# Geglu feed-forward and attention on TensorE's two row halves: rows and weights in 3.5 pieces of 128, worked in two phases

## The chip, the core and the metric

The kernel runs on one core of a Trainium2 chip. The metric is the device time of one execution in microseconds (us), as the median of several runs. Beside it there is one profiled execution, with its trace. The engines are called as in the profile: PE is TensorE's matmul, PEld its weight load, DVE VectorE, ACT ScalarE, POOL GpSimd, SP SyncE, which here only issues DMAs.

## The reference

One input `x` of 2048 rows and 448 columns goes through a layernorm without gain. The result feeds two branches, whose product is added to `x`. All inputs are bfloat16.

```python
xn = _layernorm(x)                                   # 2048 x 448
# branch A: attention, 16 query heads of 256, 8 key/value heads, the last W = 512 keys
q = (xn @ wq).reshape(B, Sq, Hq, Dh)                 # wq: 448 x 4096
scores = einsum("bhqd,bhkd->bhqk", q, k) * Dh ** -0.5
s = (softmax(scores) @ v).reshape(B, Sq, Hq * Dh) @ wo
# branch B: feed-forward, F = 1792
g = _silu((_gelu(xn @ w_gate) * (xn @ w_up)) @ w_down)
return x + s * g
```

## The kernel before

The rows are worked in four chunks (`c`) of 512, each of four tiles (`t`) of 128 rows. Two products contract over the 448 columns of `xn`: gate/up and Q. 448 is seven times 64, and so the kernel splits TensorE's 128 rows into two halves. A matmul uses 64 rows and 128 columns of the array, and the two halves run side by side on different work, each with its own PSUM bank. The transposed `xnT` therefore holds seven pieces of 64 rows, and holds each of them twice, in partitions 0 to 63 and in 64 to 127. The gate weights lie in the lower half of `wgu` and the up weights in the upper half; `wq` has one head of a pair in each half.

**Recording and order.** Every operation goes through `Rec.op` (line 65), which writes down for each engine a list in program order, and finds by keys such as `("ps", bank)` on which earlier operations it depends. Each engine runs its own list strictly in this order; a dependence on another engine becomes a semaphore wait (`emit`, line 98). A dependence of a TensorE operation on an earlier one of TensorE is left out. DMAs are issued from SP (`q1` in the profile) or POOL (`q0`), and they too wait in their issuing engine's list.

**Start.** Four loads bring the first chunk of `x`; DVE takes the statistics (L288, L289), ACT the square root (L330), DVE normalises (L294). `warm` (L303) keeps TensorE busy meanwhile with 12 matmuls of zeros. `ln_tr` transposes tile by tile on TensorE (L316), 14 half transposes per tile, each tile into a bank of its own (4 to 7), and ACT (L322) or DVE (L324) copies the bank into `xnT`. For the later chunks `ln_later` (statistics on DVE, reciprocal root on POOL, L345 and L347) and `ln_later2` (L294 twice, once for each copy, and a DMA transpose from SP) are woven into the feed-forward loop of the chunk ahead: in chunk 0 from `f` = 4 on, in chunks 1 and 2 from `f` = 1 on, alternately one of each.

**Feed-forward.** For each chunk the loop over `f` (14 blocks of 128 of the 1792 columns) calls `gate_up` (L362): 14 matmuls (L370) fill bank `s` with a gate block and bank `s + 1` with the up block; ACT takes Gelu of the first (L374) and DVE multiplies the second by it (L376), into `actT`. Three pairs of banks (0 to 5) take turns. Then `down` (L379, L382) does 4 times 14 matmuls of 448 columns into banks 6 and 7. In the last chunk `down` is deferred: its matmuls fill the first slots of attention (`fill`, line 528). Weight pieces for attention are loaded by `load_piece` from POOL, each held back until a named TensorE operation is done.

**Attention.** A step is one head of one chunk (64 steps `i`), in four tiles `t`. `scores` (L420) does two matmuls into bank 4 or 5, ACT takes exp with a row sum (L424), DVE the reciprocal and the scaling (L426, L427), and an SP DMA transposes into `pT`. `values` (L440) follows some two and a half steps later, `outproj` (L460) eight steps in groups. Every four steps `q_burst` (L398) makes Q for four heads: four times 14 matmuls (L406), each 14 copied by ACT out of two banks at once (L410). Burst 0 uses bank pairs (4, 0, 2, 0), the others (0, 2, 0, 2). It stands after the first score and values of every fourth step, and the next score follows directly.

Of the kernel before, what the change touches and what calls it, by code (L numbers as in the profile page):

```python
# [11 lines left out]
P = 128  # L12
# [10 lines left out]
class Rec:  # L23
# [41 lines left out]
    def op(self, eng, fn, r=(), w=(), dma=False, after=(), lane=None):  # L65

        o = _Op(eng, fn, dma, lane)
        deps = []
        if lane is not None:
            if lane in self.lanes:  # L70
                deps.append((self.lanes[lane], True))
            self.lanes[lane] = o
        for k in (*r, *w):
            deps += [(x, True) for x in self._touch(k)]
        for k in r:
            if k in self.writer:
                deps.append((self.writer[k], True))
        for k in w:
            if k in self.writer:
                deps.append((self.writer[k], False))  # L80
            deps += [(x, False) for x in self.readers.get(k, [])]
        deps += [(x, True) for x in after]
        for d, raw in deps:
            if d.eng == eng and not d.dma and not dma and (eng == "tensor" or not raw and eng != "gpsimd"):
                continue
            d.inc = d.waited = True
            o.deps.append(d)
        for k in r:
            self.readers.setdefault(k, []).append(o)
        for k in w:  # L90
            self.writer[k] = o
            self.readers[k] = []
        if dma:
            o.inc = True
        self.ops[eng].append(o)
        return o
# [45 lines left out]
def bass_recurrent_scan__sliding_block_cached__geglu_ffn__prompt_kernel(nc, A_x, A_k, A_v, A_wq, A_wo, B_x, B_wg, B_wu, B_wd, out):  # L142
# [6 lines left out]
    QC, TPC, HP = 512, 4, 64  # L149
    NQC = S // QC  # L150
    NT = NQC * TPC
    NK = D // HP
    NF, NJ, NE = F // P, W // P, Dh // P
    assert S % QC == 0 and D % HP == 0 and NE == 2 and NJ == 4 and Hq == 2 * Hkv and Hq % 4 == 0 and NF % 2 == 0
# [4 lines left out]
    with es:  # L159
# [20 lines left out]
        xnT, _ = sb("xnT", [P, NQC, NK, QC], BF16)  # L180
# [3 lines left out]
        wq, _ = sb("wq", [P, NK, Hkv, Dh], BF16)  # L184
        wo, _ = sb("wo", [P, Hq * NE, D], BF16)
        gu_at = off[0]
        wgu, x_at = sb("wgu", [P, NK, F], BF16)
        x4, _ = sb("x4", [P, NT, D], BF16)
        NX = 4
        xn2, d_at = sb("xn2", [P, NX, NK, 2, HP], BF16)  # L190
        wd, _ = sb("wd", [P, NF, D], BF16)
        actT, hb_at = sb("actT", [P, NF, QC], BF16)
        NHB = 4
        hb, ffn_end = sb("hb", [P, NHB, QC], BF16)

# [9 lines left out]
        while at + 2 * W <= d_at:  # L205
            t_, at = sb("pr%d" % len(pr), [P, W], BF16, at)
            pr.append(t_)
        at = hb_at
        while at + 2 * W <= ffn_end:
            t_, at = sb("pr%d" % len(pr), [P, W], BF16, at)  # L210
            pr.append(t_)
# [27 lines left out]
        dve(lambda e: e.memset(actT[:, NF - 1, :], 0.0), w=[("actT", NF - 1)])  # L239
# [9 lines left out]
        wg_v = B_wg.rearrange("(k p) f -> p k f", p=HP)  # L249
        wu_v = B_wu.rearrange("(k p) f -> p k f", p=HP)  # L250
        cuts = [0, 2, 6, 10, NF]
        fslice = {f: s for s in range(4) for f in range(cuts[s], cuts[s + 1])}

        def load_gu(s):
            a, b = cuts[s] * P, cuts[s + 1] * P
            dma("sync", wgu[0:HP, :, a:b], wg_v[:, :, a:b], w=[("wgu", 0, s)])
            dma("sync", wgu[HP:P, :, a:b], wu_v[:, :, a:b], w=[("wgu", 1, s)])
# [6 lines left out]
        for sl in range(4):  # L264
# [4 lines left out]
        for c in range(2, NQC):  # L269
# [5 lines left out]
        wq_v = A_wq.rearrange("(k p) (g two m) -> p k g two m", p=HP, two=2, m=Dh)  # L275
        pieces = [(wq[lo * HP:(lo + 1) * HP, k, :, :], wq_v[:, k, :, lo, :], ("wq", lo, k))
                  for k in range(NK) for lo in range(2)]
# [13 lines left out]
        def ln_norm(t, copies=2):  # L291
            s = t % NX
            for o in range(copies):
                dve(lambda e, o=o: e.tensor_scalar(  # L294
                    xn2[:, s, :, o, :], x4[:, t, :].rearrange("p (k d) -> p k d", k=NK), mv[:, t, 0:1],
                    rstd[:, t:t + 1], op0=ALU.subtract, op1=ALU.mult),
                    r=[("x4", t), ("mv", t), ("rstd", t)], w=[("xn2", s, o)])

        def warm(n):

            def run(e):
                for _ in range(n):
                    ins = e.matmul(bank(3), lhsT=actT[:, NF - 1, 0:P], rhs=actT[:, NF - 1, :], start=True, stop=True)  # L303
# [3 lines left out]
        def ln_tr(t):  # L307
            parts = ((act, 4),), ((dve, 5),), ((act, 6),), ((dve, 7),)
            parts = [(eng, b, 0, NK) for eng, b in parts[t]]
            for eng, b, a, z in parts:  # L310
                tp = bank(b).bitcast(BF16)

                def tr(e, tp=tp, a=a, z=z):
                    for k in range(a, z):
                        for lo in (0, HP):
                            ins = e.transpose(tp[lo:lo + HP, (k - a) * P:(k - a + 1) * P], xn2[:, t, k, 0, :], ident[:, :])  # L316
                    return ins
                pe(tr, r=[("xn2", t, 0), ("ident",)], w=[("ps", b)])
                dst = xnT[:, 0, a:z, t * P:(t + 1) * P]
                src = tp[:, 0:(z - a) * P].rearrange("p (k q) -> p k q", q=P)  # L320
                if eng is act:
                    act(lambda e, dst=dst, src=src: e.activation(dst, src, ACT.Copy), r=[("ps", b)], w=[("xnT", 0, t, a)])  # L322
                else:
                    dve(lambda e, dst=dst, src=src: e.tensor_copy(dst, src), r=[("ps", b)], w=[("xnT", 0, t, a)])  # L324
# [7 lines left out]
        for a in range(0, TPC, 2):  # L332
            dve(lambda e, a=a: e.reciprocal(rstd[:, a:a + 2], std[:, a:a + 2]),
                r=[("std", a)], w=[("rstd", a), ("rstd", a + 1)])
            ln_norm(a, 1)
            ln_norm(a + 1, 1)
        warm(12)
        for t in range(TPC):
            ln_tr(t)
        xn0 = [("xnT", 0, t, 0) for t in range(TPC)]  # L340
# [9 lines left out]
        def ln_later2(t):  # L350
            c, t4 = divmod(t, TPC)
            ln_norm(t)
            dmaT(xnT[:, c, :, t4 * P:(t4 + 1) * P], xn2[:, t % NX, :, :, :].rearrange("p k a d -> p (k a d)"),
                 r=[("xn2", t % NX, 0), ("xn2", t % NX, 1)], w=[("xnT", c, t4)])

        def xn(c):
            return [("xnT", c, t) for t in range(TPC)] if c else xn0
# [4 lines left out]
        def gate_up(c, f):  # L362

            n = c * NF + f
            s = 2 * (n % NGB)

            def run(e):
                for k in range(NK):
                    for b, lo in ((s, 0), (s + 1, HP)):
                        ins = e.matmul(bank(b), lhsT=wgu[lo:lo + HP, k, f * P:(f + 1) * P],  # L370
                                       rhs=xnT[lo:lo + HP, c, k, :], start=k == 0, stop=k == NK - 1)
                return ins
            pe(run, r=xn(c) + [("wgu", 0, fslice[f]), ("wgu", 1, fslice[f])], w=[("ps", s), ("ps", s + 1)])
            act(lambda e: e.activation(hb[:, n % NHB, :], bank(s), ACT.Gelu_apprx_tanh),  # L374
                r=[("ps", s)], w=[("hb", n % NHB)])
            dve(lambda e: e.tensor_tensor(actT[:, f, :], bank(s + 1), hb[:, n % NHB, :], ALU.mult),  # L376
                r=[("ps", s + 1), ("hb", n % NHB)], w=[("actT", f)])

        def down(c, t, part=range(NF)):  # L379
            b = (6, 7, 7, 2)[t] if c == NQC - 1 else 6 + t % 2  # L380
# [15 lines left out]
        def q_burst(G):  # L396

            c, h0 = divmod(4 * G, Hq)  # L398
            for n in range(4):
                hp, e_ = divmod(n, 2)  # L400
                s, i = 2 * (n % 2) if G else (4, 0, 2, 0)[n], (4 * G + 2 * hp) % 6

                def run(e, hp=hp, e_=e_, s=s):
                    for k in range(NK):
                        for b, lo in ((s, 0), (s + 1, HP)):
                            ins = e.matmul(bank(b), lhsT=wq[lo:lo + HP, k, h0 // 2 + hp, e_ * P:(e_ + 1) * P],  # L406
                                           rhs=xnT[lo:lo + HP, c, k, :], start=k == 0, stop=k == NK - 1)
                    return ins
                pe(run, r=xn(c) + [("wq", lo, k) for lo in range(2) for k in range(NK)], w=[("ps", s), ("ps", s + 1)])
                act(lambda e, e_=e_, s=s, i=i: e.activation(  # L410
                    qT[:, i:i + 2, e_, :], psum[:, s * 512:(s + 2) * 512].rearrange("p (a q) -> p a q", a=2), ACT.Copy),
                    r=[("ps", s), ("ps", s + 1)], w=[("qT", i, e_), ("qT", i + 1, e_)])
# [93 lines left out]
        for c in range(NQC):  # L506
            lead = 4 if c == 0 else 1
            for f in range(NF):
                gate_up(c, f)
                if c + 1 < NQC and lead <= f < lead + 2 * TPC:  # L510
                    t, half = divmod(f - lead, 2)
                    (ln_later2 if half else ln_later)((c + 1) * TPC + t)
                if f >= 9 and f % 2:
                    load_piece()
            for g in ((0, 1), (2, 3, 4), (5, 6, 7), ())[c]:
# [12 lines left out]
        for d, slots in ((0, range(0, 4)), (1, range(4, 12)), (2, range(16, 20)), (3, range(20, 24))):  # L528
# [4 lines left out]
        for i in range(NI):  # L533
            for t in range(TPC):
                scores(i, t)
                if 4 * i + t in fill:
                    down(NQC - 1, *fill[4 * i + t])
                if t % 2 == 0 and 4 * i + t >= 10:
                    values(*pv.pop(0))
                if 6 <= i and t % 2:  # L540
                    outproj(*outs[0], range(2 * t - 2, 2 * t + 2))
                    if t == TPC - 1:
                        outs.pop(0)
                if t == 0 and i % 4 == 3 and i + 1 < NI:
                    q_burst(i // 4 + 1)
            if 7 <= i and (i - 7) % 3 == 0 and (i - 7) // 3 < NT:
# [43 lines left out]
```

## Time and profile before

| | |
|---|---|
| median of 3 runs | 560.89 us (560.74 to 561.54) |
| the profiled execution | 561.18 us |
| its span in the trace | 559.4 us |
| granted TensorE clock | 1.00 |
| PE busy | 549.0 us (98%) in 3499 records |
| DVE, ACT, POOL busy | 322.9, 296.1, 90.1 us |
| chain that ended last | PE 95% |
| DMA | 58.83 MB, mean 105 GB/s |

All times in a profile line are counted from the start of the span. In a line of groups stand the line of the kernel, the engine, the operation, the tiles out<-in with their sizes and the count; then the busy time in us, the mean of one in ns, and the idle time of the engine just before it with what ended that. In a line of the timeline stand the start and the length in us, then the operation and its count; the square bracket has the idle time before it. Matmuls are pipelined: the time of one in the groups (376 ns) is longer than its share in a dense sequence. The 1.78 us between span and time lie outside the program's instructions.

### The profile page before, as it was taken

How to read it: one execution, taken by the hardware profiler on the slowest of the kernel's cores; microseconds unless marked ns; L12 is line 12 of the kernel's file. 1: busy time of each engine (PE TensorE's matmuls, PEld its weight loads, DVE VectorE, ACT ScalarE, POOL GpSimd, SP SyncE). 2: the span in 40 equal slices, each digit the busy share in tenths (PEclk: the TensorE clock that was granted, in tenths of full speed). 3: DMA queues.
4: the chain of work that ended last, by engine and by line, in shares of the span. 5: the costliest groups of instructions: out<-in, count | busy, mean ns of one | idle time of the engine just before them, and what ended most of it. 6: DMA issues, size and time to landing. Idle time of an engine off the chain costs nothing.

```text
span 559.4 us, 9865 instructions
## 1 busy us (share of the span) xinstructions
PE 549.0 (98%) x3499; PEld 257.2 (46%) x3532; DVE 322.9 (58%) x835; ACT 296.1 (53%) x673; POOL 90.1 (16%) x125
## 2 busy tenths in 40 slices
PE   7999999999999999999999999999999999999997
PEld 3544444444444444444444444444444444444445
DVE  5636446143464847474846657484747484755674
ACT  4324233247655565556565656656565656565641
POOL 0232323200000111013501101232100021400023
PEclk9999999999999999999999999999999999999999
DMA  8994746972453435353664344445535353645352
GB/s 193 276 191 86 138 102 136 247 137 65 94 85 68 97 64 99 69 91 64 143 98 94 73 86 71 81 84 137 101 67 99 63 95 71 147 79 101 70 92 52
DMA packets 169552, 58.83 MB, mean 105 GB/s; under 512 B 160160, under 2 KB 166432, under 8 KB 169504
## 3 DMA queue, kind: packets, MB, share of 16 engines
q1 hardware_dynamic: 166208, 45.50, 44.2%
q0 software_dynamic: 3152, 12.65, 8.9%
q8 instruction: 28, 0.46, 0.4%
q14 instruction: 20, 0.16, 0.1%
q10 hardware_dynamic: 144, 0.06, 0.0%
HBM read 17.92 MB, written 1.84 MB: 35 GB/s over the span
## 4 chain that ended last, share of the span: by engine, by line
PE 95%; DMA 1%; DVE 1%; issue 1%; SPq 1%; ACT 0%
PE ps L440 20%; PE ps L420 19%; PE ps L406 18%; PE ps L460 16%; PE ps L370 15%; PE ps L382 8%; DMA wgu<-in_B_w_up_dram 1%; SPq L233 1%; DVE tmp L469 0%; DVE ofin L471 0%; DVE pr L427 0%; DVE oT L446 0%; DVE rden L426 0%; ACT pr L424 0%
## 5 line engine op out<-in xcount | busy, mean ns | idle before, releaser
L424 ACT ACTIVATE pr<-ps 128x512 bf16<-128x512 f32 x256 | 152.8, 597 | 116.6 <-PE ps L420 112.5
L420 PE MATMUL ps<-kT,qT 128*128 128x512 bf16 x481 | 145.4, 379 | 3.3 <-issue 2.5
L440 PE MATMUL ps<-pT,V 128*128 128x512 bf16 x510 | 130.8, 379 | 0.6 <-DVE rden L426 0.4
L426 DVE RECIPROCAL rden<-den 128x1 f32<-128x1 f32 x256 | 41.5, 162 | 152.4 <-ACT pr L424 134.3
L460 PE MATMUL ps<-wo,oT 128*128 128x448 bf16 (+1 forms) x536 | 116.3, 344 | 0.0
L427 DVE TENSOR_SCALAR pr<-pr,rden 128x512 bf16<-128x512 bf16 x256 | 106.4, 416 | 9.0
L406 PE MATMUL ps<-xnT,wq 64*128 64x512 bf16 x896 | 99.5, 376 | 0.0
L410 ACT ACTIVATE qT<-ps 128x1024 bf16<-128x1024 f32 x64 | 65.5, 1024 | 49.8 <-PE ps L406 49.8
L370 PE MATMUL ps<-xnT,wgu 64*128 64x512 bf16 x784 | 85.5, 376 | 1.0 <-ACT xnT L322 0.8
L446 DVE CAST oT<-ps 128x512 bf16<-128x512 f32 x124 | 84.6, 682 | 0.6 <-PE ps L440 0.5
L440 PEld LDWEIGHTS ps<-pT,V 128*128 128x128 bf16 x512 | 49.9, 98 | 60.8 <-issue 1.2
L460 PEld LDWEIGHTS ps<-wo,oT 128*128 128x128 bf16 x536 | 52.3, 98 | 51.1
L420 PEld LDWEIGHTS ps<-kT,qT 128*128 128x128 bf16 x512 | 48.5, 98 | 57.1 <-issue 7.3
L376 DVE TENSOR_TENSOR actT<-ps,hb 128x512 bf16<-128x512 f32 x56 | 38.1, 685 | 57.5 <-ACT hb L374 55.7
L406 PEld LDWEIGHTS ps<-xnT,wq 64*128 64x128 bf16 x896 | 42.4, 94 | 55.9 <-DVE acc L481 4.2
L374 ACT ACTIVATE hb<-ps 128x512 bf16<-128x512 f32 x56 | 33.4, 597 | 51.8 <-PE ps L370 51.8
L370 PEld LDWEIGHTS ps<-xnT,wgu 64*128 64x128 bf16 x784 | 39.2, 94 | 46.5 <-issue 2.5
L424 ACT ACTIVATION_READ_ACCUMULATOR pr<-ps 128x1 f32 x256 | 49.9, 195 | 0.0
L500 POOL TENSOR_SCALAR tmp<-tmp 128x448 f32<-128x448 f32 x16 | 9.1, 572 | 233.9 <-ACT tmp L499 233.9
L382 PE MATMUL ps<-wd,actT 128*128 128x448 bf16 x224 | 46.2, 353 | 0.1
L485 POOL TENSOR_TENSOR tmp<-acc,gy 128x448 f32<-128x448 f32 x16 | 16.6, 1035 | 123.2 <-DVE acc L481 123.2
L382 PEld LDWEIGHTS ps<-wd,actT 128*128 128x128 bf16 x224 | 21.7, 98 | 22.2 <-issue 1.3
(43 smaller groups left out, 171.7 us busy)
## 6 DMA issues: line engine op xcount, KB each, us to landing
pT<-pr SPq DMA_TRANSPOSE x256, 2.4
wq<-in_A_wq_dram POOLq DMA_DIRECT2D x14, 256.0 KB, 4.3
wo<-in_A_wo_dram POOLq DMA_DIRECT2D x4, 896.0 KB, 10.1
V<-in_A_v_cache_dram POOLq DMA_DIRECT2D x4, 512.0 KB, 5.8
xr<-in_A_x_dram POOLq DMA_DIRECT2D x4, 448.0 KB, 4.8
wd<-in_B_w_down_dram SPq DMA_DIRECT2D x1, 1568.0 KB, 17.6
wgu<-in_B_w_gate_dram SPq DMA_DIRECT2D x3, 448.0 KB, 10.3
wgu<-in_B_w_up_dram SPq DMA_DIRECT2D x3, 448.0 KB, 11.8
```

The lines of the kernel that those rows point to most:

```text
L370: ins = e.matmul(bank(b), lhsT=wgu[lo:lo + HP, k, f * P:(f + 1) * P], rhs=xnT[lo:lo + HP, c, k, :], start=k == 0, stop=k == NK - 1)
L376: dve(lambda e: e.tensor_tensor(actT[:, f, :], bank(s + 1), hb[:, n % NHB, :], ALU.mult), r=[("ps", s + 1), ("hb", n % NHB)], w=[("actT", f)])
L382: pe(lambda e, f=f: e.matmul(bank(b, D), lhsT=actT[:, f, t * P:(t + 1) * P], rhs=wd[:, f, :], start=f == 0, stop=f == NF - 1), r=[("actT", ...
L406: ins = e.matmul(bank(b), lhsT=wq[lo:lo + HP, k, h0 // 2 + hp, e_ * P:(e_ + 1) * P], rhs=xnT[lo:lo + HP, c, k, :], start=k == 0, stop=k == ...
L410: act(lambda e, e_=e_, s=s, i=i: e.activation(qT[:, i:i + 2, e_, :], psum[:, s * 512:(s + 2) * 512].rearrange("p (a q) -> p a q", a=2), AC ...
L420: ins = e.matmul(bank(b), lhsT=qT[:, i % 6, k, t * P:(t + 1) * P], rhs=kT[:, g, k, :], start=k == 0, stop=k == NE - 1)
L424: act(lambda e: e.activation(pr[s][:, :], bank(b), ACT.Exp, scale=scale, accum_out=den[:, s:s + 1]), r=[("ps", b)], w=[("pr%d" % s,), ("de ...
L426: dve(lambda e: e.reciprocal(rden[:, s:s + 1], den[:, s:s + 1]), r=[("den", s)], w=[("rden", s)])
L427: dve(lambda e: e.tensor_scalar(pr[s][:, :], pr[s][:, :], rden[:, s:s + 1], None, op0=ALU.mult), r=[("pr%d" % s,), ("rden", s)], w=[("pr%d ...
L440: ins = e.matmul(bank(b), lhsT=V[:, j, g, e_ * P:(e_ + 1) * P], rhs=pT[:, i % NPT, j, :], start=j == 0, stop=j == NJ - 1)
L446: dve(lambda e: e.tensor_copy(dst, bank(b)), r=[("ps", b)], w=[key])
L460: ins = e.matmul(bank(b, D)[:, lo:hi], lhsT=oT[G % 2][:, idx, t * P:(t + 1) * P], rhs=wo[:, h0 * NE + idx, lo:hi], start=idx == 0, stop=id ...
```

## The change

- `xnT` holds four pieces: three of 128 rows, and the last 64 rows twice. Gate and up weights become `wg` and `wu`, three pieces of 128 rows, with the last 64 rows in `wg6` and `wu6`: an even column block in the lower partitions, an odd one in the upper. `wq` and `wq6` likewise.
- `two_blocks` does a unit of two column blocks in two phases. In phase 0 the lower row half works on block 0 and the upper on block 1, with all four pieces (8 matmuls); in phase 1 the halves exchange blocks, over three pieces (6 matmuls). Phase 1 of a unit is issued after phase 0 of the next, and waits for its own phase 0 by a semaphore (`hard`).
- `gate_up` has 14 units in a chunk, even ones of two gate blocks and odd ones of two up blocks. ACT's Gelu and DVE's product each take 1024 columns, over two banks. `hb` has two double buffers.
- `wg`, `wu` come in three slices (two, two and three block pairs) from SP; `wg6`, `wu6` from POOL, the first two block pairs at once, and the other five after phase 1 of unit 0.
- At the start five transposes per tile instead of 14, into banks 6 and 7 in turn, copies of 512 columns, 48 warm-up matmuls of 128 columns, and a Gelu of one column ahead of ACT's copies.
- The later layernorm writes 448 + 64 columns, and its DMA transpose has 512.
- `q_burst` takes three pairs of banks (0, 2, 4, 0) in the same two phases. In a step with a burst, the second tile's score comes after the output projection. The filling `down` pieces come last in their slot, and those of tiles 2 and 3 move from slots 16 to 23 to slots 12 to 19. There are 12 `pr` buffers.

The diff, cut to its core:

```diff
-    def op(self, eng, fn, r=(), w=(), dma=False, after=(), lane=None):
+    def op(self, eng, fn, r=(), w=(), dma=False, after=(), lane=None, hard=()):
...
+        for d in hard:
+            d.inc = d.waited = True
+            o.deps.append(d)
...
-        cuts = [0, 2, 6, 10, NF]
-        fslice = {f: s for s in range(4) for f in range(cuts[s], cuts[s + 1])}
+        cuts = [0, 2, 4, NF2]
+        jslice = {j: s for s in range(3) for j in range(cuts[s], cuts[s + 1])}
...
+        def load_gu6(a, b, after=()):
+            for _, w6, name, _, src in w_gu:
+                for h in range(2):
+                    dma("gpsimd", w6[h * HP:(h + 1) * HP, a:b, :], src[h, :, a:b, :],
+                        w=[(name + "6", h, a > 0)], after=after)
...
-        def ln_norm(t, copies=2):
+        def ln_norm(t, twice=True):
             s = t % NX
...
+            for lo, a in ((0, 0), (D, D - HP))[:1 + twice]:
+                dve(lambda e, lo=lo, a=a: e.tensor_scalar(
+                    xn2[:, s, lo:lo + D - a], x4[:, t, a:D], mv[:, t, 0:1], rstd[:, t:t + 1],
...
+            b = 6 + t % 2
+            tp = bank(b).bitcast(BF16)
+            def tr(e):
+                for k in range(KF):
+                    e.transpose(tp[:, k * P:(k + 1) * P], xn2[:, t, k * P:(k + 1) * P], ident[:, :])
+                for lo in (0, HP):
+                    ins = e.transpose(tp[lo:lo + HP, KF * P:(KF + 1) * P], xn2[:, t, KF * P:D], ident[:, :])
+                return ins
...
-        warm(12)
+        act(lambda e: e.activation(small[:, 3:4], small[:, 0:1], ACT.Gelu_apprx_tanh), r=[("eps",)], w=[("warm2",)])
+        warm(48)
         for t in range(TPC):
             ln_tr(t)
+            ln_copy(t)
...
+        def two_blocks(ph, c, s, cols, w, w6, keys, q0=0, q1=QC):
+            def run(e):
+                for k in range(KF + 1 - ph):
+                    for lo in (0, HP):
+                        m = (lo > 0) ^ ph
+                        lhsT = w[lo:lo + HP, k, cols[m]:cols[m] + P] if k < KF else w6[lo:lo + HP, :]
+                        ins = e.matmul(bank(s + m)[:, q0:q1], lhsT=lhsT, rhs=xnT[lo:lo + HP, c, k, q0:q1],
+                                       start=ph == 0 and k == 0, stop=ph == 1 and k == KF - 1)
+                return ins
+            hard = [phase0[s]] if ph else []
+            phase0[s] = pe(run, r=xn(c)[q0 // P:q1 // P] + keys, w=[("ps", s), ("ps", s + 1)], hard=hard)
...
-        def gate_up(c, f):
+        def gate_up(c, f, ph, q0=0, q1=QC):
+            j, up = divmod(f, 2)
             n = c * NF + f
-            s = 2 * (n % NGB)
+            s, h = 2 * (n % NGB), (n // 2) % NHB
...
+            two_blocks(ph, c, s, (2 * j * P, (2 * j + 1) * P), w, w6[:, j, :], keys, q0, q1)
+            if ph == 0 or q1 < QC:
+                return
+            two = psum[:, s * 512:(s + 2) * 512].rearrange("p (a q) -> p a q", a=2)
+            if up:
+                dve(lambda e: e.tensor_tensor(actT[:, 2 * j:2 * j + 2, :], two, hb[:, h, :, :], ALU.mult),
+                    r=[("ps", s), ("ps", s + 1), ("hb", h)], w=[("actT", 2 * j), ("actT", 2 * j + 1)])
+            else:
+                act(lambda e: e.activation(hb[:, h, :, :], two, ACT.Gelu_apprx_tanh),
+                    r=[("ps", s), ("ps", s + 1)], w=[("hb", h)])
...
-                s, i = 2 * (n % 2) if G else (4, 0, 2, 0)[n], (4 * G + 2 * hp) % 6
+                s, i, h = 2 * (n % 3), (4 * G + 2 * hp) % 6, h0 + 2 * hp
...
+            for n in range(5):
+                if n < 4:
+                    part(n, 0)
+                if n:
+                    part(n - 1, 1)
...
-            for f in range(NF):
-                gate_up(c, f)
+            for f in range(NF + 1):
+                if f < NF:
+                    gate_up(c, f, 0)
+                if f:
+                    gate_up(c, f - 1, 1)
...
+                if c == 0 and f == 1:
+                    load_gu6(2, NF2, after=[R.ops["tensor"][-1]])
...
-        for d, slots in ((0, range(0, 4)), (1, range(4, 12)), (2, range(16, 20)), (3, range(20, 24))):
+        for d, slots in ((0, range(0, 4)), (1, range(4, 12)), (2, range(12, 16)), (3, range(16, 20))):
...
-                scores(i, t)
-                if 4 * i + t in fill:
-                    down(NQC - 1, *fill[4 * i + t])
+                late = t == 1 and i % 4 == 3
+                if not late:
+                    scores(i, t)
                 if t % 2 == 0 and 4 * i + t >= 10:
                     values(*pv.pop(0))
...
+                if late:
+                    scores(i, t)
                 if t == 0 and i % 4 == 3 and i + 1 < NI:
                     q_burst(i // 4 + 1)
+                if 4 * i + t in fill:
+                    down(NQC - 1, *fill[4 * i + t])
```

## The prediction

> **What bounds the kernel now.** I read the page first: its busy times and its chain by engine.
>
> ```profile
> PE 549.0 (98%) x3499; PEld 257.2 (46%) x3532; DVE 322.9 (58%) x835; ACT 296.1 (53%) x673; POOL 90.1 (16%) x125
> PE 95%; DMA 1%; DVE 1%; issue 1%; SPq 1%; ACT 0%
> ```
>
> TensorE sets the end. Next, the full chain in order of time says whether its pace has slack.
>
> ```profile
> 41.68 21.26 PE ps L370 x196
> 126.85 6.04 PE ps L406 x56
> ```
>
> 21.26/196 = 0.1085 us for a matmul with 64 rows; a unit of 14 takes 1.52, eight 0.87, six 0.65. No wait shows between units: evictions are hidden. So only fewer matmuls, a shorter start or tail, or new waits can move the time. The groups give what evictions cost:
>
> ```profile
> L410 ACT ACTIVATE qT<-ps 128x1024 bf16<-128x1024 f32 x64 | 65.5, 1024 | 49.8 <-PE ps L406 49.8
> L376 DVE TENSOR_TENSOR actT<-ps,hb 128x512 bf16<-128x512 f32 x56 | 38.1, 685 | 57.5 <-ACT hb L374 55.7
> ```
>
> Last, the timeline of the first 22 us, for latencies and the layernorm chain:
>
> ```profile
> 0.85 0.27 DVE L239 MEMSET actT<- 128x256 uint32 x1 [0.85 <-PEq L575]
> 1.18 0.13 PEld L303 LDWEIGHTS ps<-actT 128*128 128x128 bf16 x2 [1.18 <-DVE actT L239]
> ...
> 7.09 1.94 ACT L322 ACTIVATE xnT<-ps 128x896 bf16<-128x896 bf16 x2 [0.94 <-PE ps L316]
> ...
> 9.23 2.73 PEld L370 LDWEIGHTS ps<-xnT,wgu 64*128 64x128 bf16 x28 [0.90 <-ACT xnT L322]
> 9.26 3.20 PE L370 MATMUL ps<-xnT,wgu 64*128 64x512 bf16 x28 [0.77 <-ACT xnT L322]
> ...
> 10.98 0.60 ACT L374 ACTIVATE hb<-ps 128x512 bf16<-128x512 f32 x1 [0.65 <-PE ps L370]
> ...
> 12.67 9.67 PE L370 MATMUL ps<-xnT,wgu 64*128 64x512 bf16 x88 [0.22 <-DMA wgu<-in_B_w_up_dram]
> ...
> 18.73 0.62 DVE L288 BATCH_NORM_STATS2 stats<-x 128x6 f32<-128x448 bf16 x1
> ...
> 20.63 0.92 DVE L294 TENSOR_SCALAR xn<-x,mv,rstd 128x448 bf16<-128x448 bf16 x2 [0.31 <-POOL rstd L347]
> 21.47 0.68 DVE L376 TENSOR_TENSOR actT<-ps,hb 128x512 bf16<-128x512 f32 x1
> ```
>
> The first unit is issued by 9.26 + 1.52 = 10.78 and ACT starts at 10.98: TensorE to eviction 0.20. The memset ends at 1.12 and TensorE starts at 1.18: eviction to TensorE 0.06 (0.20 by ACT's 9.03 to 9.23). From a tile's statistics to its normalisation, 18.73 to 20.63, are 1.90 us, by way of POOL.
>
> **TensorE's own work.** Nothing goes. 3.5 pieces of 128 sound like half of 7 of 64, but each half is a matmul of its own: 8 in phase 0 and 6 in phase 1 are the 14 of before. Gate/up stays at 784, Q at 896, with the same switches between 64 and 128 rows. Cost 0.
>
> **Waits on TensorE itself.** Each second phase waits for its first: 4x14 + 16x4 = 120 waits. Queued behind each are six matmuls, and everything after them on TensorE; the evictions wait for those. Between a first phase and its second lies another unit's phase, 0.65 us at least, against 0.20 + 0.06 to signal. Covered: 0 (at most 0.26 each uncovered; no row shows TensorE waiting for itself; nothing is gained).
> The Trainium skill, "TensorEngine Tiling (Array Packing)", Gotcha 1, says row tiles cannot use one PSUM bank at once and that software must synchronise: a reason for these waits; no run here shows it.
>
> **Start.** On ACT a Gelu table load and dummy (1.28 + 0.20) now stand ahead of the first xnT copy: square root done 6.15, copy 7.66 to 8.26 (0.60 for 512, L374). Transposes use two banks instead of four, so tile 2 waits for that copy: from 8.32, five transposes some 0.25; tile 3's follow to 8.82, DVE's copy 9.02 to 9.44 (619 ns for 896 columns, some 0.42 for 512), first gate at 9.5. That loses 0.25, and the DMA wait at 12.67 (0.22 and restart) goes, as weights arrive for 128 partitions: net 0. Bounds: -0.7 if the copies follow the last normalisation (7.86) directly, +0.5 if all latencies are 0.20.
> The warm-up is 48 matmuls of 128 columns instead of 12 of 512: the same columns.
> A rule speaks against this: the Trainium skill, "TensorE: Matmul & The Clock Gate", Part 1, has the clock halved again after a window of some 3.4 us without activity. In before, only transposes lie between 5.38 and 9.26, and the granted clock stayed 1.00; I add nothing (by the rule, an estimated 1.7 us for one window at half clock).
>
> **The last weight rows (wg6, wu6).** Four small POOL DMAs come early enough. The other four wait for phase 1 of unit 0; behind them in POOL's queue stand only the layernorm steps and later weight pieces, due later. Unit 4 needs the second of them. From that phase's end TensorE has 2x0.87 + 2x0.65 = 3.04 us of work. POOL wakes after 0.20, issues the first in 0.64 (wq 0.68, xr 0.55); the second must then land. Nearest rows:
>
> ```profile
> wq<-in_A_wq_dram POOLq DMA_DIRECT2D x14, 256.0 KB, 4.3
> x<-in_A_x_dram SPq DMA_DIRECT2D x4, 112.0 KB, 2.2
> ```
>
> For 80 KB on POOL's slower path, amid wd's transfer, I take 3.3, between both. Stall 0.84 + 3.3 + 0.06 - 3.04 = 1.2; bounds 0.1 and 2.2.
> The Trainium skill, "DMA: Bandwidth & Descriptors", Anatomy of one DMA, fits 2.0 us plus bytes over 436 KB per us, an estimate of 2.2 here and a stall of 0.1. The trace's 256 KB took 4.3 instead of the fit's 2.6, so I stay with the rows.
>
> **Evictions of 1024 columns.** A pair of banks is now one block pair: ACT's Gelu 1.02 (L410), DVE's product 0.685 for 512 columns and, at the 1.06 ns per column between its 448 and 512 rows (617, 685), 1.22 for 1024. DVE is busy less (28x(2x0.685 - 1.22) = 4.2 us, off the path), but releases banks later. Unit f+3 needs unit f's banks; between phase 1 of f and phase 0 of f+3 lie 8 + 6 matmuls, 1.52. Gelu needs 0.20 + 1.02 + 0.06 = 1.28: hidden. The product needs 0.20 + 1.22 + 0.06 = 1.48: a margin of 0.04, or -0.10 with 0.20 back. The up-units 1 to 9 of chunks 1 to 3 (15) can stall: 0 to 0.12 each. I take 0.04: 0.6; bounds 0 and 1.8.
>
> **Layernorm among them.** In chunk 0 DVE's order is product, statistics, normalisation, product: a chain of 1.22 + 1.90 + 0.42 + about 0.1 (the repeated 64 columns) = 3.64 per tile against two units, 3.04. Unit 5's product starts 3.84 after unit 3's end and finishes at 5.06; unit 8 should start at 4.56, starts at 5.12: 0.56. Then 0.60 for units 10 and 12; unit 11's product falls before the down projection's 10.7 us, hidden. Sum 1.8; bounds 1.1 (back-to-back overlap of 0.08 at each step) and 2.5 (64 columns as dear as 448). In chunks 1 and 2 the order is product, normalisation, statistics, and the 1.90 lies beside a unit: 0.
>
> **Q bursts.** Burst 0 starts in banks 0, 1, whose Gelu (unit 12 of the last chunk) needs 1.28 with only phase 1 of unit 13 (0.65) for cover: 0.63. Before, it began in banks 4, 5. At its end the first score needs bank 4, copied from the third pair: 1.28 against 0.65 and a switch of 0.1: 0.53. Together 1.2, bounds 1.0 and 1.4. In the other 15 bursts the first pair's copy (1.28) has 1.52; the late score has the output projection (0.76) or a down piece (0.57) besides, so 1.28 stands against 1.32 or more; exp after it is released 0.2 early: 0. Moved fill pieces meet free banks: 0. SP's queue only gets smaller transposes.
>
> **Sum.** 0 + 1.2 + 0.6 + 1.8 + 1.2 = 4.8 on the profiled execution's own 561.18 us (span 559.4 and 1.78 around it): 566.0. The median of before lies 0.29 lower, so 565.7. Low ends together give +1.5 (562.4), high ends +8.4 (569.3).
>
> **Rivals.** First, the waits on TensorE cost something each. The chunk that started after a wait took 18.31 for 168, 0.07 over the others' pace; 120x0.07 = 8.4 on top: 574. For it: weight loads usually run ahead, and a wait may stop that. Against: units with satisfied waits show no gap now. It decides once signalling takes over 0.65.
> Second, not slower: the start wins. Its place is between the last normalisation (7.86) and the first gate (9.26), its price -0.7 (tile 3's five transposes some 0.25, DVE's copy 0.42, signals 0.3: first gate at 8.85, and no wait at 12.67). It decides the sign once the stalls sum to under 0.7, that is with a layernorm chain under 3.04 and wg6 landing 2.1 us after its issue: 560.2. For it: 36 transposes of some 36 ns (2.02/56) and 0.32 of ACT's copy go. Against it: the table load and the two banks stand in its way, and 1.90 of the layernorm chain is measured.
> Third, only burst 0's waits remain and all else is hidden: 562.1, within 0.2% (1.1 us, about what a measurement can tell from no change).
> Fourth, the part of wg6 and the clock gate fail badly (landing 5.4 as the first wq piece, plus a throttled window): some 569.5.
>
> **How the numbers follow.** Forecast 0.66 (all slower); waits 0.10, slower; not slower 0.12, of which faster by over 0.2% 0.07 and within 0.2% 0.05; only burst 0 0.04, within; fourth 0.08, slower. Faster 0.07, same 0.09, slower 0.84. The range 562.0 to 569.5 holds the forecast and the third and fourth, and leaves out the waits and most of the not slower.
>
> **What would show it.** After: L396 with 1680 matmuls at 0.1085; TensorE idle on DMA wg6 near 15 us; on DVE actT three times some 0.6 between 18 and 30; on ACT before burst 0 and its first score; first gate near 9.5. No idle in chunk 0, or gaps at each second phase, would make the prediction wrong.

## The result, and the profile after

The changed kernel takes 573.83 us (median of 6 runs, 571.62 to 575.38) against 560.82 us for the kernel before (6 runs): 1.0229 times the time, 95% interval 1.0208 to 1.0250. It is slower, as forecast, but by 13 us instead of 4.8, and above the upper end of the range, 569.5. The profiled execution took 573.68 us with a span of 571.9 us, 12.5 us more than that of before on both counts. All differences below are taken between these two profiled executions unless a median is named.

The page of the changed kernel, its busy times, the granted clock in 40 slices of 14.3 us, and the chain by engine:

```profile
PE 556.7 (97%) x3499; PEld 259.7 (45%) x3532; DVE 314.8 (55%) x807; ACT 288.7 (50%) x646; POOL 93.7 (16%) x133
PEclk8799999999999999999999999999999999999999
PE 93%; DVE 3%; DMA 2%; issue 1%; ACT 1%; POOL 0%; DVEq 0%
```

TensorE has as many records as before, 3499, but 7.7 us more busy time, and the clock row dips below 9 in the first two slices alone. So TensorE did the same work, part of it at a lower clock, and all of that within the first 29 us. DVE and DMA have a larger share of the chain. In order of time (start, length, what):

```profile
15.06 6.94 DMA wg<-in_B_w_gate_dram
...
29.44 1.22 DVE actT L417
33.09 1.13 DVE actT L417
36.64 1.14 DVE actT L417
...
41.67 10.70 PE ps L426 x56
52.37 21.27 PE ps L396 x196
73.64 10.70 PE ps L426 x56
84.34 21.26 PE ps L396 x196
...
136.95 1.03 ACT hb L420
138.07 1.24 DVE actT L417
139.35 4.73 PE ps L396 x42
144.10 1.03 ACT qT L450
```

Two things are to be read here. Chunks 1 and 2 take 21.27 and 21.26 us for their gate/up and 10.70 for `down`, as in the kernel before: the two phases, their waits and the wide evictions cost nothing where nothing else disturbs them. And the loss lies at two places: the first `down` starts at 41.67 instead of 30.98 (10.7 us), and at the first Q burst, where ACT and DVE stand in the chain (1.7 us: from the start of chunk 3 to the first score 29.19 instead of 27.46). After that 0.1 is left to explain: 10.7 + 1.7 = 12.4 of 12.5.

**Chunk 0.** The timeline of the changed kernel from its first gate matmul (start, length, operation, in brackets the idle time before it):

```profile
9.84 1.49 PE L396 MATMUL ps<-xnT,wg 64*128 64x512 bf16 x8 [0.57 <-ACT xnT L350]
14.37 1.36 POOL L242 DMA_DIRECT2D wg<-in_B_w_gate_dram  x2 [10.02 <-PE ps L396]
22.13 1.89 PE L396 MATMUL ps<-xnT,wg 64*128 64x512 bf16 x8 [5.04 <-DMA wg<-in_B_w_gate_dram]
33.00 1.22 DVE L417 TENSOR_TENSOR actT<-ps,hb 128x1024 bf16<-128x1024 f32 x1
34.27 1.04 PE L396 MATMUL ps<-xnT,wg 64*128 64x512 bf16 x8 [0.34 <-DVE actT L417]
```

The second `wg6` load was issued at 15.06 and landed at 22.00. The last matmul before it ended at 17.09 in the trace; counted at the pace of a dense sequence, the work before it was done at 16.92, so that TensorE had no work for 5.2 us. The windows of the same trace (PE, PEld, DVE, ACT and POOL busy, then the granted clock, DMA share and GB/s) show what went with it:

```profile
10.00:12.00 2.00, 2.00 (x14) 0.87 (x12) 0.00 (x0) 0.00 (x0) 0.00 (x0) 0.57 1.04 380
12.00:14.00 2.00, 2.00 (x14) 0.92 (x12) 0.00 (x0) 0.00 (x0) 0.00 (x0) 0.57 1.06 369
14.00:16.00 2.00, 2.00 (x22) 1.04 (x19) 0.38 (x1) 1.02 (x1) 1.63 (x3) 1.00 1.11 342
20.00:22.00 2.00, 0.00 (x0) 0.00 (x0) 0.00 (x0) 0.00 (x0) 0.00 (x0) 0.63 1.02 261
22.00:25.00 3.00, 2.87 (x14) 1.22 (x16) 0.00 (x0) 0.00 (x0) 0.00 (x0) 0.50 0.24 66
25.00:28.00 3.00, 3.00 (x20) 1.34 (x18) 1.94 (x3) 0.07 (x1) 0.51 (x2) 0.61 0.00 0
28.00:32.00 4.00, 4.00 (x40) 1.90 (x38) 2.55 (x5) 1.97 (x2) 0.71 (x3) 1.00 0.16 33
```

The clock was halved twice. (A window at 0.57 is one that was at half clock for 86% of its length.) The first stretch, some 10.3 to 13.7, lies over the first units: 50 matmuls from 9.84 to 16.92 took 7.08 us instead of 50 x 0.1085 = 5.43, a loss of 1.65. The second began within the stall, at about 20.5, and lasted until about 27.4: 36 matmuls from 22.13 to 28.58 took 6.45 instead of 3.9, a loss of 2.55. DMA stood at its full share (1.02 to 1.11) until the awaited piece had landed. The end of chunk 0 shows the layernorm chain: products of DVE start 3.55 us apart (29.44, 33.00, 36.55, 40.11), where two units take 3.02.

**Burst 0.** The timeline there:

```profile
136.95 1.02 ACT L420 ACTIVATE hb<-ps 128x1024 bf16<-128x1024 f32 x1 [2.00 <-PE ps L396]
138.03 1.04 PE L396 MATMUL ps<-xnT,wq 64*128 64x512 bf16 x8 [0.47 <-ACT hb L420]
138.07 1.23 DVE L417 TENSOR_TENSOR actT<-ps,hb 128x1024 bf16<-128x1024 f32 x1 [1.41 <-ACT hb L420]
139.35 5.35 PE L396 MATMUL ps<-xnT,wq 64*128 64x512 bf16 x48 [0.29 <-DVE actT L417]
145.49 0.38 PE L466 MATMUL ps<-kT,qT 128*128 128x512 bf16 x1 [0.78 <-ACT qT L450]
```

The first eight matmuls wait for Gelu; the next wait for the product of unit 13, and that product itself could not start before the same Gelu had ended. The first score then waits 0.78 for the copy (0.16 before).

### The profile page after: what moved, and what is told of

It is laid out like the page before. It is cut to its first block, busy times and chain, and to the rows that moved or that the text cites. A ratio compares the mean times of both kernels' runs of the same rounds, so it can differ in the third digit from the quotient of the medians.

```text
span 571.9 us, 9714 instructions
## 1 busy us (share of the span) xinstructions
PE 556.7 (97%) x3499; PEld 259.7 (45%) x3532; DVE 314.8 (55%) x807; ACT 288.7 (50%) x646; POOL 93.7 (16%) x133
## 4 chain that ended last, share of the span: by engine, by line
PE 93%; DVE 3%; DMA 2%; issue 1%; ACT 1%; POOL 0%; DVEq 0%
PE ps L396 31%; PE ps L486 19%; PE ps L466 19%; PE ps L506 16%; PE ps L426 7%; DMA wg<-in_B_w_gate_dram 1%; DVE actT L417 1%; DVE stats L312 1%; DVE tmp L515 0%; DVE ofin L517 0%; DMA x<-in_A_x_dram 0%; ACT L363 0%; POOL rstd L374 0%; DVE mv L313 0%; ACT xnT L350 0%
## 5 line engine op out<-in xcount | busy, mean ns | idle before, releaser
L466 PE MATMUL ps<-kT,qT 128*128 128x512 bf16 x480 | 142.6, 379 | 2.4 <-ACT qT L450 0.8
L450 ACT ACTIVATE qT<-ps 128x1024 bf16<-128x1024 f32 x64 | 63.8, 1022 | 57.1 <-PE ps L396 55.5
L417 DVE TENSOR_TENSOR actT<-ps,hb 128x1024 bf16<-128x1024 f32 x28 | 34.3, 1223 | 75.7 <-PE ps L396 70.6
L506 PEld LDWEIGHTS ps<-wo,oT 128*128 128x128 bf16 x536 | 51.1, 98 | 53.8 <-issue 5.9
L466 PEld LDWEIGHTS ps<-kT,qT 128*128 128x128 bf16 x512 | 49.9, 98 | 54.2 <-issue 1.2
L420 ACT ACTIVATE hb<-ps 128x1024 bf16<-128x1024 f32 x28 | 28.6, 1023 | 67.3 <-PE ps L396 67.3
L396 PE MATMUL ps<-xnT,wg 64*128 64x512 bf16 x392 | 50.2, 388 | 6.3 <-DMA wg<-in_B_w_gate_dram 5.0
L396 PE MATMUL ps<-xnT,wu 64*128 64x512 bf16 x392 | 50.0, 390 | 0.0
L396 PEld LDWEIGHTS ps<-xnT,wg 64*128 64x128 bf16 x392 | 18.5, 96 | 32.6 <-issue 8.8
```

The source lines that it names most:

```text
L396: ins = e.matmul(bank(s + m)[:, q0:q1], lhsT=lhsT, rhs=xnT[lo:lo + HP, c, k, q0:q1], start=ph == 0 and k == 0, stop=ph == 1 and k == KF - 1)
L417: dve(lambda e: e.tensor_tensor(actT[:, 2 * j:2 * j + 2, :], two, hb[:, h, :, :], ALU.mult), r=[("ps", s), ("ps", s + 1), ("hb", h)], w=[( ...
L420: act(lambda e: e.activation(hb[:, h, :, :], two, ACT.Gelu_apprx_tanh), r=[("ps", s), ("ps", s + 1)], w=[("hb", h)])
L450: act(lambda e: e.activation(qT[:, i:i + 2, e_, :], psum[:, s * 512:(s + 2) * 512].rearrange("p (a q) -> p a q", a=2), ACT.Copy), r=[("ps" ...
L466: ins = e.matmul(bank(b), lhsT=qT[:, i % 6, k, t * P:(t + 1) * P], rhs=kT[:, g, k, :], start=k == 0, stop=k == NE - 1)
L506: ins = e.matmul(bank(b, D)[:, lo:hi], lhsT=oT[G % 2][:, idx, t * P:(t + 1) * P], rhs=wo[:, h0 * NE + idx, lo:hi], start=idx == 0, stop=id ...
```

## The experiments

**First question: where do the 10.7 us of chunk 0 come from?** My theory after the result: the late load of `wg6` and `wu6` costs its wait and, by the pause, a second stretch at half clock. Rivals: POOL's way of loading is slow as such; or the waits between the phases cost 0.07 each, the first rival of the prediction, whose 574 is just what was measured.

*All weight rows at once.* The five late block pairs are loaded at the start:

```diff
         load_gu6(0, 2)
+        load_gu6(2, NF2)
...
-                if c == 0 and f == 1:
-                    load_gu6(2, NF2, after=[R.ops["tensor"][-1]])
```

> Base is the changed kernel (573.83 median; 12.5 us over before in the profile). Theory D (a late DMA and the clock): wg6 and wu6 are all loaded at the start, so the 5.2 us without work before unit 4 goes, and with it the second stretch at half clock (2.55 us); the layernorm chain gets back the one stall that the slow clock hid (+0.5). 573.8 - 5.2 - 2.5 + 0.5 = 566.6, between 565 and 568.5. Rival W (the 120 waits of TensorE on itself cost some 0.07 each, 8.4 in all, and the missing time only shows up elsewhere): the time falls by no more than 4, to 570 or above. Rival C (POOL's path is slow whatever else runs): the loads that are now early still land some 7 us after their issue, which unit 4 does not feel.

Measured: 566.22 us (10 runs, 564.12 to 567.51), ratio 1.0084 (1.0060 to 1.0108). That is 7.6 us less than the changed kernel, by four late loads moved to the start. In its profile the stall is gone, and what remains in chunk 0 is three stalls on DVE like this one (the others at 27.03 and 30.59), and one throttled stretch over the first units:

```profile
23.48 1.04 PE L397 MATMUL ps<-xnT,wg 64*128 64x512 bf16 x8 [0.36 <-DVE actT L418]
```

Three times a spacing of 3.56 instead of 3.02 is 1.6 us for the layernorm chain.

*Late load, empty queue.* `wg6` and `wu6` stay late, but the 1.57 MB of `wd` and the last two chunks of `x` move behind them in time:

```diff
-        dma("sync", wd[:, :, :], ...)
-        for c in range(2, NQC):
-            load_x(c)
...
+                if c == 0 and f == 5:
+                    dma("sync", wd[:, :, :], ..., after=[R.ops["tensor"][-1]])
+                    for c2 in range(2, NQC):
+                        load_x(c2)
```

> wg6 and wu6 stay late, as in the changed kernel, but wd and the last two loads of x are issued only once unit 4 is done. Theory D says that the four POOL loads landed 7 us after issue because these 2.4 MB filled the DMA engines: the landing falls to 3 to 4 us, the wait before unit 4 from 5.2 to some 1 to 1.8, the second throttled stretch goes: 573.8 - 3.8 - 2.5 + 0.5 = 568, between 566 and 570. Rival C (POOL's path is slow by itself, by the many pieces of 256 bytes): the landing stays at 6 to 7 us and the time at 573 or more.

Measured: 567.34 us (7 runs), ratio 1.0092 (1.0056 to 1.0127). The DMA issues (KB each, median us to landing) of this kernel, and under them those of the changed kernel:

```profile
wg<-in_B_w_gate_dram POOLq DMA_DIRECT2D x2, 80.0 KB, 2.8
wu<-in_B_w_up_dram POOLq DMA_DIRECT2D x2, 80.0 KB, 2.5
```

```profile
wg<-in_B_w_gate_dram POOLq DMA_DIRECT2D x2, 80.0 KB, 7.0
wu<-in_B_w_up_dram POOLq DMA_DIRECT2D x2, 80.0 KB, 6.8
```

The same loads, at the same place in POOL's queue, landed in 2.5 to 2.8 us instead of 6.8 to 7.0 once SP's queue was empty (38 GB/s over 14 to 23 us instead of 299). TensorE's wait fell to 0.71. So it was the traffic of SP's queue, not POOL's way.

*The waits, put into the kernel before.* Each of its sequences of 14 matmuls is recorded as eight and six, and the six wait by a semaphore for the six of the sequence before: 119 waits of the same kind.

```diff
+        def two_parts(run, r, s):
+            pe(lambda e: run(e, 0, 4), r=r, w=[("ps", s), ("ps", s + 1)])
+            o = pe(lambda e: run(e, 4, NK), r=r, w=[("ps", s), ("ps", s + 1)], hard=last[-1:])
+            last.append(o)
```

> The kernel before with 119 waits of TensorE on itself: each unit of 14 is recorded as 8 and 6, and the 6 wait for the 6 of the unit before, with the 8 in between, as in the changed kernel. Theory D: no cost, 560.9, within 0.3. Rival W: 119 x 0.07 = 8.3 more, 569.

Measured: 560.73 us (10 runs, 560.52 to 561.38), ratio 0.9989 (0.9969 to 1.0009). 8.3 us would have been 1.5%. The rival named the right time for the wrong reason: a wait on TensorE's own earlier work, with eight matmuls between, costs nothing that shows. In the changed kernel there are six at the least, and its chunks 1 and 2 show no cost either.

**Second question: the other parts, one by one.** *Burst 0 in banks that are free.* Its four units of 14 matmuls take the bank pairs 6, 4, 0, 2 instead of 0, 2, 4, 0:

```diff
-                s, i, h = 2 * (n % 3), (4 * G + 2 * hp) % 6, h0 + 2 * hp
+                s, i, h = 2 * (n % 3) if G else (6, 4, 0, 2)[n], (4 * G + 2 * hp) % 6, h0 + 2 * hp
```

> Only the bank pairs of burst 0 are changed, to 6, 4, 0, 2, so that it starts in banks that are long free and the first score's bank 4 is copied second. Theory D with burst 0's stalls at 1.8 us as read in the trace: no idle time of TensorE from the last gate/up unit to the first score; 573.8 - 1.7 = 572.1 (the throttled stretches make single runs scatter by 2 us). Rival W: the copies come no earlier since TensorE's own waits pace the burst: no change in that stretch.

Measured: 572.43 us (4 runs), ratio 1.0188 (1.0141 to 1.0236), 1.4 under the changed kernel by medians. In its chain the last chunk's gate/up and the burst are one piece:

```profile
116.73 27.30 PE ps L396 x252
```

From the start of chunk 3 to the first score it takes 144.19 - 116.73 = 27.46 us, as in the kernel before, the changed kernel 145.49 - 116.30 = 29.19: 1.7 us lay in the choice of banks.

*Layernorm ordered as in chunks 1 and 2.* On top of the early load, the statistics of the next tiles begin one unit earlier, so that product, normalisation and statistics follow in that order:

```diff
-            lead = 4 if c == 0 else 1
+            lead = 3 if c == 0 else 1
```

> Base is e1 (566.22; all last weight rows early). In chunk 0 the layernorm for the next chunk starts one unit earlier (lead 3 instead of 4), so that DVE's order is product, normalisation, statistics, and the 1.90 us by way of POOL lie beside a unit. Theory D (a chain of 3.55 per tile against 3.02 of matmuls): the three stalls of 0.53 before units 8, 10 and 12 go, 566.2 - 1.6 = 564.6 (563.5 to 565.7 with the clock's scatter). Rival E (the products of 1024 columns are too late by themselves): stalls remain at every second unit, 565.5 or above.

Measured: 565.77 us (4 runs, 564.96 to 566.22), ratio 1.0082 (1.0067 to 1.0098), just above the expected range. Its chain:

```profile
10.04 23.99 PE ps L397 x196
34.03 10.70 PE ps L427 x56
```

The three stalls are gone, gate/up of chunk 0 runs as one piece. But 23.99 is still 2.7 over 21.26, and the windows of this trace show a granted clock of 0.50 from 10 to 14 us, and less than 1.00 from about 8.6 to 15.4: all four runs had a mean clock of 0.994 to 0.996, where seven of the early-load kernel's ten had 0.996 or 0.997. At 0.994 the first took 565.62 to 566.22 (three runs), the early-load kernel 567.45 (one run). So the order is worth some 1.5 us, and the clock took most of it back.

*TensorE kept busy during the transposes.* On top of the early load, matmuls of zeros follow the transposes of the second tile (seven) and of the fourth (five):

```diff
             ln_copy(t)
+            if t % 2:
+                warm(7 if t == 1 else 5)
```

> e1 with 7 matmuls of zeros after the second tile's transposes and 5 after the fourth's, where TensorE was idle (0.9 and 0.6 us). Theory D: TensorE's idle time ahead of the first gate unit is what halves the clock from about 10 us on; granted clock 1.00 from the grant on, median 566.2 - 1.7 = 564.5, like the one run of e1 at clock 1.000 (564.12). Rival F (the clock is taken back whatever happens there, or the transposes do not matter): the clock stays below 1.00 in most runs and the median at 566.

Measured: 564.77 us (4 runs, 564.66 to 564.83), ratio 1.0067 (1.0054 to 1.0081), with a clock of 1.000 in all four and 1.00 in every window of the profile. The spread of 3.4 us in the early-load kernel is reduced to 0.2. The one early-load run at a clock of 1.000 took 564.12, 0.65 less; that the zeros cost this is not shown, since the first gate unit starts at 9.88 in both traces.

*The start with four banks.* On top of the early load, the transposes go to banks 4 to 7 and the Gelu ahead of ACT's copies is left out:

```diff
-            b = 6 + t % 2
+            b = 4 + t
...
-        act(lambda e: e.activation(small[:, 3:4], small[:, 0:1], ACT.Gelu_apprx_tanh), ...)
```

> e1 with the four transposed tiles in banks 4 to 7 and without the Gelu dummy ahead of ACT's copies, as in the kernel before. Theory D: the first gate unit starts at 8.6 to 8.9 instead of 9.88, and the shorter gap leaves the clock alone: 566.2 - 1.1 - 1.7 = 563.4 (563 to 564.6). Rival G (the start is set by weights that land): first gate at 9.4 or later, 565.5 or above.

Measured: 564.06 us (4 runs, 563.56 to 564.77), ratio 1.0056 (1.0042 to 1.0070). In the trace the first gate unit starts at 8.98 instead of 9.88, a little after the 8.6 to 8.9 expected, and earlier than in the kernel before (9.26). The prediction had named this start (8.85) as its second rival, and had named rightly what stands in its way: the table load and the two banks.

**Third question: what is the two-phase form worth when nothing is in its way?** *All parts together:* early load, layernorm order, start with four banks, burst 0 in free banks.

> e1, e5, e7 and e3's banks together: last weight rows early, layernorm order, start, burst 0. Theory D says that nothing but these parts separates the changed kernel from the one before: 566.2 - 1.6 - 1.1 - 1.7 - 1.7 = 560.1, between 559.7 and 561, so as fast as before or up to 0.2% faster. Rival H (the two phases cost something of their own): 562 or above.

Measured: 560.96 us (11 runs, 560.51 to 562.63), ratio 1.0005 (0.9996 to 1.0014). Its first `down` starts at 30.30, 0.68 earlier than before, and all of this is lost at one wait that I had not seen coming, in TensorE's timeline:

```profile
142.29 1.02 PE L486 MATMUL ps<-pT,V 128*128 128x512 bf16 x4 [0.68 <-issue]
```

My reading was that the first values come too early: the change moved the filling `down` pieces behind them, and they no longer give the exp and transposes of the first tiles their time. The order cannot be all of it: the changed kernel and the one with burst 0 in free banks have the same order, and wait 0.23 and 0.26 us there. What made it 0.68 here is not known; the profile names nothing ("issue").

*Fill pieces ahead of the values* again, except where a burst stands:

```diff
+                burst = t == 0 and i % 4 == 3 and i + 1 < NI
+                if 4 * i + t in fill and not burst:
+                    down(NQC - 1, *fill[4 * i + t])
                 if t % 2 == 0 and 4 * i + t >= 10:
                     values(*pv.pop(0))
```

> e8 with the filling down pieces back between a tile's score and its values, as in the kernel before, except in the slot of a burst. In e8's trace the first down projection starts 0.68 us earlier than before, yet the span is the same: TensorE waits 0.68 at the first values (L486) for a transposed pT, since nothing stands between. Theory D: that wait goes and the median falls from 560.96 by 0.5 to 560.4 (560.0 to 560.8). Rival J (the gain is lost wherever DVE or the transposes set the pace, not in the order of the list): 560.9, with idle time at a later values.

Measured: 560.62 us (11 runs, 560.38 to 562.64), ratio 0.9997 (0.9988 to 1.0006); of the wait 0.20 is left in the trace. The 0.3 us under the kernel with all parts are not clear of the scatter: the two intervals overlap. One of these 11 runs and three of the 11 before had a clock of 0.997, and these four are the four over 562.4.

*The same with more zeros* at the warm-up and after the last transposes:

```diff
-        warm(48)
+        warm(52)
...
+        warm(5)
```

> e9 with 52 warm-up matmuls instead of 48 and 5 more after the last transposes, where TensorE had been idle for 0.6 us. Theory D: the runs of e8 at a granted clock of 0.997 (562.4, 3 of 11) no longer occur; median as e9 or 0.1 below, highest run under 561.3. Rival F (the clock is taken back whatever TensorE does there): some runs stay 1.5 us longer, or the added matmuls delay the first gate unit by 0.2.

Measured: 560.72 us (11 runs, 560.40 to 561.61), ratio 0.9996 (0.9987 to 1.0005). No run had a clock below 0.999, and the highest is 1 us lower. In the trace the first gate comes 0.27 later (9.24 instead of 8.97), but so do the first transposes, ahead of the five added matmuls (6.81 instead of 6.54), because the normalised rows they wait for are later; so the zeros are not shown to cost it. That none would exceed 561.3 was missed by 0.3. So with every obstacle away the new form is level with the kernel before; no version beat it by anything that can be measured.

## Why the prediction was wrong

Right in direction, wrong in size. By its own terms, in us:

| term | predicted | measured |
|---|---|---|
| TensorE's own work | 0 | 0 |
| waits between phases | 0 | 0 |
| start | 0 | 0.2 |
| wait for `wg6`, `wu6` | 1.2 (0.1 to 2.2) | 5.2 |
| clock gate | 0 | 4.2 |
| evictions of 1024 columns | 0.6 | 0 |
| layernorm chain | 1.8 | 1.1 |
| burst 0 | 1.2 | 1.7 |
| sum | 4.8 | 12.4 |

**The step that failed first is the landing of `wg6`.** I took 3.3 us, between a 256 KB load of POOL (4.3) and a 112 KB load of SP (2.2), and set the bounds by these rows. Both are medians over all such loads of the run. This one was issued when `wd` and two chunks of `x` were queued on all DMA engines, and the windows of before already showed a DMA share of 1.04 to 1.16 from 6 to 22 us. With 6.94 in the place of 3.3 the same sum gives 0.84 + 6.94 + 0.06 - 3.04 = 4.8, near the 5.2 measured. I wrote "amid wd's transfer" and did not price it; the run with the empty queue shows that this was the whole of the error: there the same loads took 2.5 to 2.8, less than the 3.3.

**The second is the clock gate, taken at 0.** It cost 1.65 at the start and 2.55 after the stall. That the clock of before stayed at 1.00 although only transposes lay between 5.38 and 9.26 (3.88 us) I took to hold for the changed start too. In the changed kernel the warm-up ended at 6.28 and the first gate came at 9.84, only 3.56 us later, and the clock fell. In the run with the empty queue, whose start is the same, the pause in the trace was longer, 4.61 us (5.42 to 10.03), and the clock stayed at 1.00. So the length of the pause does not decide alone. The warm-up of these two traces, the changed kernel first:

```profile
0.98 5.30 PE L327 MATMUL ps<-actT 128*128 128x128 bf16 x48 [0.98 <-DVE actT L248]
0.98 4.44 PE L324 MATMUL ps<-actT 128*128 128x128 bf16 x48 [0.98 <-DVE actT L248]
```

The same 48 matmuls stand 0.107 us apart to the end in the first; in the second they are 0.107 apart until 4.4 us and 0.056 after. (The granted clock of the windows reads 1.00 there in both, so for these first microseconds the pace is to be trusted and not the clock.) Full pace was thus reached at another moment in each execution. The Trainium skill, "TensorE: Matmul & The Clock Gate", Part 1, says that the clock is halved after a window of some 3.4 us without activity, and that these windows run freely and do not start anew with a kernel. The traces agree: in the changed kernel the clock fell or rose at about 10.3, 13.7, 20.5 and 27.4 us, once or twice 3.4 us apart. The second stretch is a consequence of the first error: with the stall gone, it is gone from the traces of the early load and of the empty queue. The fourth rival had both mechanisms together, but with one throttled window and a landing of 5.4, and so stopped at 569.5.

**In burst 0 one dependence was missed.** I priced the entry by the Gelu of unit 12 (0.63; measured about 0.6) and the exit by the third copy (0.53; measured 0.6 more than before). Between them the second unit of the burst waits for the product of unit 13, which waits for that same Gelu: some 0.45 more. Merging two evictions into one makes a second engine's wide eviction start where the first one's ends, and at the end of the last chunk no unit is left to cover it.

**What held.** The waits on TensorE itself: the experiment on the kernel before shows that they cost nothing. The 0.07 us on which the first rival built was a misreading. The chain's piece of 18.31 runs to 30.98, but the next sequence had started by then, as the timeline of before shows. The chain and the timeline:

```profile
12.67 18.31 PE ps L370 x168
```

```profile
30.91 1.31 PE L382 MATMUL ps<-wd,actT 128*128 128x448 bf16 x6
```

From 12.67 to 30.91 are 18.24, which is 168 times 0.1086, the pace of all others. The chain per tile: 3.64 forecast, 3.55 measured; of the three stalls forecast only two were seen in the changed kernel, where the wait and the half clock had made the first units late, and with the load early there are three. The wide product: its margin of 0.04 a unit, which I had charged with 0.6 in all, was never used up. The start held in its sum and not in its parts: the first gate came at 9.84 instead of 9.5, 0.58 after that of before, since a tile's five transposes took some 0.44 (8.31 to 8.75) and not 0.25; the wait for weights that went, at 12.67 in before, was worth 0.4.

What stays open: what decides whether one execution is throttled in the first units and the next is not. In the four traces with a throttled start full pace came after 5.2 us or not within the warm-up; in six of the eight others it came before 5.0. The two exceptions are the kernel before with added waits (about 5.6) and the one with the fill pieces first, whose gate already starts at 8.97. More zeros went with fewer throttled runs (none of 15 in the two kernels that have them; 4 of 22 in the two all-parts kernels without), but the kernel with the four-bank start alone had none in 4 either, and two of 58 runs of the kernel before also lay at 566 with a clock of 0.997. The moment at which full pace comes was not controlled.

## What to carry to other kernels

Price a transfer by a row that met the same load: if the DMA share is at 1 when it is issued, count the bytes queued ahead of it and not its own (here it landed as the share fell to 0.24, at 22 us), or issue it so early that nothing waits for it (the loads moved to the start still took 7.1 to 7.9 us to land). A pause of TensorE can cost twice, once for itself and once for slow matmuls behind it: pauses of 3.6 to 4.6 us with only transposes in them did so in some executions and not in others, so one profile at a clock of 1.00 does not show that a kernel is safe; the stall of 5 us was followed by half clock in both traces that have it. When two evictions become one, follow the longer hold on the banks to the ends of each loop, where the usual cover is missing.

## What the runs showed of the hardware

The throttle comes in portions. Mean clocks of the runs lie near 1.000, 0.997, 0.994, 0.991 and 0.988, and the times go with them: the changed kernel took 571.62 at 0.994, 573.60 to 574.27 at 0.991 and 575.38 at 0.988. A step of 0.003 of 565 us is 1.7 us lost, or 3.4 us at half clock, which is the length of the first stretch in the trace; the second, 6.9 us, is two of them. In the trace with burst 0 in free banks it is the other way round, about 6.8 us (8.9 to 15.7) at the start and 3.5 (22.5 to 26.0) after the stall. The two runs of the kernel before at 0.997 do not fit: they were some 5 us longer than its others, so they lost more than this step, and what else slowed them is not known.

The loads of the changed kernel, most of them into 128 partitions, ran faster than those of before, into 64: between 6 and 14 us DMA moved 219 to 238 GB/s in the kernel before, 341 to 380 in the changed one, at about the same DMA share. The rows loaded are also longer, and no run separates the two. The first gate does not profit, since it waits for the layernorm's copies and not for weights: the profile names ACT's, but the copy that ended last, at 9.73, is DVE's of the fourth tile. The one wait for weights in chunk 0 of before, some 0.4 us at 12.67, is gone.
